# Part of one chunk of the output weights given to the first six DMA engines, with the softmax sums moved to ScalarE and four idle matmuls removed

## The chip, the cores and the metric

One Trainium2 chip, one core of it. The metric is device microseconds (us) of one execution. All numbers of runs are of executions that the record counts as fast (label2 is a single run, its state unknown); the times of one kernel are compared with runs of the kernel before made on the same chip in the same rounds. A ratio is the mean time of one kernel's fast runs over that of the other's of the same rounds, so it is not quite the ratio of the medians that are quoted beside it.

## The reference

One decode step of attention with a cached context, mixed with a gated MLP. What matters here is only the last step: the attention output `o` (32 heads of 128) times the output weights `wo`.

```python
# x: 1 x 1024;  k_cache, v_cache: 4 groups x 65536 x 128;  wo: 4096 x 1024, all bfloat16
scores = jnp.einsum('bhqd,bhkd->bhqk', q, k) * Dh ** (-0.5)
p = _softmax(scores, axis=-1)
o = jnp.einsum('bhqk,bhkd->bhqd', p, v)
a = o.transpose(0, 2, 1, 3).reshape(B, Sq, Hq * Dh) @ wo
out = g * a + (1 - g) * b          # g: a gate of x; b: the MLP branch
```

The inputs are 162 MB, each byte used once, so the kernel is a stream of loads with work hidden behind it.

## The kernel before

All loads go out from one queue (SyncE), in the order in which they are needed, into a ring of slots; a load waits until its slot has been used. The output weights come last, as four chunks of 1024 rows; the fourth is cut in three pieces so that little work is left after the last bytes.

```python
    def rows(w, i, c):          # chunk i: 128 partitions, c rows of w behind each other in each
        return w[128 * c * i:128 * c * (i + 1), :].rearrange("(p c) n -> p (c n)", c=c)
    ...
    WO_CUT = [(0, 5), (5, 7), (7, 8)]
    for i in range(3):
        load([("wo", i, 0)], rows(A_wo, i, 8), WO_AT[i])
    for c0, c1 in WO_CUT:
        load([("wo", 3, c0)], rows(A_wo, 3, 8)[:, DO * c0:DO * c1], WO_AT[3] + DO * c0)
```

The sum of the softmax of a group is a float32 product over two halves, and `spin(n)` runs n matmuls whose result nobody reads, to keep TensorE's clock up while it waits:

```python
    def out_first(g):
        def f(e):
            for h in range(2):
                ins = e.matmul(mb[:, 0:1], bm, lp[:, 2 * g + h:2 * g + h + 1], start=(h == 0), stop=(h == 1))
            return ins
    ...
    out_first(3)
    wo_rows(0)                  # chunk 0: 16 matmuls into scp
    out_rest(3)
    wo_rows(1)
    spin(4)
    spread(scp, [KSC(0)], False)   # a ScalarE copy of 1.0 us, then 16 small matmuls
    spin(3)
    wo_piece(2)                 # 64 matmuls
    spin(3)
    for c0, c1 in WO_CUT:
        wo_piece(3, c0, c1)     # 40, 16 and 8 matmuls
```

Of the kernel before, what the change touches and what calls it, by code (L numbers as in the profile page):

```python
# [8 lines left out]
ACTF = mybir.ActivationFunctionType  # L9
# [8 lines left out]
class Recorder:  # L18
# [8 lines left out]
        self.dma_count = {}  # L27
        self.ahead = 0

    def op(self, eng, fn, r=(), w=(), dma=None):  # L30
        o = Op()
        o.eng, o.fn, o.inc, o.count = eng, fn, False, 0
        o.dma = None
        deps = {}
        for k in r:
            if k in self.writer:
                deps[id(self.writer[k])] = (self.writer[k], True)
        for k in w:
            if k in self.writer:
                deps.setdefault(id(self.writer[k]), (self.writer[k], False))  # L40
            for x in self.readers.get(k, ()):
                deps.setdefault(id(x), (x, False))
        o.deps = list(deps.values())
        for k in r:
            self.readers.setdefault(k, []).append(o)
        for k in w:
            self.writer[k] = o
            self.readers[k] = []
        if dma is not None:
            self.dma_count[dma] = self.dma_count.get(dma, 0) + 16  # L50
            o.dma = (dma, self.dma_count[dma])
        o.idx = len(self.ops)
        self.ops.append(o)
        return o
# [40 lines left out]
    def emit(self, nc):  # L95
        waits = self.plan()
        sems = {e: nc.alloc_semaphore("eng_" + e) for e in self.ENGINES}
        dsem = {k: nc.alloc_semaphore("dma_%s" % k) for k in self.dma_count}
        final = {k: v for k, v in self.dma_count.items()}

        def run(eng, handle):
            for o, ws in zip(self.ops, waits):
                if o.eng != eng:
                    continue
                for d in ws:
                    if d.dma:
                        handle.wait_ge(dsem[d.dma[0]], d.dma[1])
                    else:
                        handle.wait_ge(sems[d.eng], d.count)
                last = o.fn(handle)  # L110
                if o.dma:
                    last.then_inc(dsem[o.dma[0]], 16)
                elif o.inc:
                    last.then_inc(sems[eng], 1)

        body = nc.cur_bb.bb
        gate = next(i for i, x in enumerate(body.instructions)
                    if isinstance(x, mybir.InstDrain) and x.engine == mybir.EngineType.SP)
        first = len(body.instructions)
        run("SP", nc.sync)  # L120
        nc.sync.wait_ge(dsem["out"], final["out"])
        made = list(body.instructions)
        moved = made[first:first + self.ahead]
        assert all(isinstance(x, mybir.InstDMACopy) for x in moved)
        body.instructions = made[:gate] + moved + made[gate:first] + made[first + self.ahead:]
        run("POOL", nc.gpsimd)
        run("PE", nc.tensor)
        run("ACT", nc.scalar)
        run("DVE", nc.vector)


def bass_gated_mix__gqa_block_cached__mixer_gmlp__decode_kernel(
# [19 lines left out]
    DO = A_wo.shape[1]  # L152
# [32 lines left out]

    for name, n in [
        ("RING", NSUB * SUB), ("KT", NKT * 4096), ("SC", NSC * 2048), ("PSB", 2 * 1024), ("PTSB", 2 * 1024),
        ("QPAD", 4 * QP), ("IDB", 128), ("BM", 256), ("SEL", 16 * 32),
        ("M16", 32), ("MQ", 32), ("XT", KC), ("WB", 2), ("WBB", 4), ("ONEB", 128),
        ("MAXC", 2 * total), ("LP", 2 * total), ("COLS", 2 * 64), ("DM", 64), ("ONES", 256), ("QALL", 128), ("OVZ", 32 * OC + 31), ("E4Z", 128), ("MHALF", 4),  # L190
        ("YB", FC), ("OROW", QW),
    ]:
        region(name, n)
    NA = (cur + 63) // 64 * 64
# [2 lines left out]
    def ab(name, n, o=0):  # L197
        return arena[:, OFF[name] + o:OFF[name] + o + n]

    def af(name, n, o=0):  # L200
        return arena[:, OFF[name] + 2 * o:OFF[name] + 2 * (o + n)].bitcast(F32)
# [11 lines left out]
    mhalf = af("MHALF", 2)  # L213
    yb, ovz, orow = ab("YB", FC), ab("OVZ", 32 * OC + 31), ab("OROW", QW)
    e4z = af("E4Z", 63)
    dm = af("DM", 32)
    psb, psb2 = ab("PSB", 1024), ab("PSB", 2048)
    osc, ot = ab("PSB", 512), af("PSB", 128, 256)
    col = lambda i: colt[:, i:i + 1]
# [3 lines left out]
    def gcol(g, i):  # L223
        return col(C_G4 + 12 * g + i)
# [25 lines left out]
    def mm(e, loaded, *a, **kw):  # L250

        if not loaded:
            return e.matmul(*a, **kw)  # L253
        with nc.discard():
            one = e.matmul(*a, **kw).ins  # L255
        return e.add_instruction(dataclasses.replace(one, name=nc.get_next_instruction_name(), ldweights=False))
# [7 lines left out]
    P("POOL", lambda e: e.affine_select(out=idf, in_=idf, compare_op=ALU.not_equal, fill=1.0, base=0,  # L264
                                        pattern=[[-1, 128]], channel_multiplier=1), r=["idf"], w=["idf"])
    P("POOL", lambda e: e.tensor_copy(idb, idf), r=["idf"], w=["idb"])
    P("POOL", lambda e: e.memset(qpad, 0.0), w=["qpad"])
    P("POOL", lambda e: e.memset(orow, 0.0), w=["orow"])
    P("POOL", lambda e: e.memset(ovz, 0.0), w=[("ovec", g) for g in range(G)])
    P("POOL", lambda e: e.memset(e4z, 0.0), w=["e4"])  # L270
    P("POOL", lambda e: e.memset(ones, 1.0), w=["ones"])
    P("POOL", lambda e: e.memset(oneb, 1.0), w=["oneb"])
    P("DVE", lambda e: e.memset(mb, 0.0), w=["mb"])
# [26 lines left out]
    def load(keys, src, off):  # L300

        n = len(stream)
        w = src.shape[1]
        for i, key in enumerate(keys):
            place[key] = (n, off + i * (w // len(keys)), w // len(keys))
        stream.append((keys, off, src))

    def rows(w, i, c):

        return w[128 * c * i:128 * c * (i + 1), :].rearrange("(p c) n -> p (c n)", c=c)  # L310
# [18 lines left out]
    def load_v2(n, off):  # L329
        load([("v", n), ("v", n + 1)], kv(A_v_cache, n, True), off)  # L330

    load([("wq", 0)], rows(A_wq, 0, 8), VB)
    load_k2(0, 0)
    load([("win", 0)], rows(B_w_in, 0, 8), VB)
# [13 lines left out]
    load([("v", 15)], kv(A_v_cache, 15), VB + SUB)  # L348
    WO_AT = [0, 8 * DO, 16 * DO, 24 * DO]
    WO_CUT = [(0, 5), (5, 7), (7, 8)]  # L350
    for i in range(3):
        load([("wo", i, 0)], rows(A_wo, i, 8), WO_AT[i])
    for c0, c1 in WO_CUT:
        load([("wo", 3, c0)], rows(A_wo, 3, 8)[:, DO * c0:DO * c1], WO_AT[3] + DO * c0)
# [14 lines left out]
    def issue():  # L369

        while issued[0] < len(stream):
            n = issued[0]
            keys, off, src = stream[n]
            w = src.shape[1]
            gr = grains(off, w)
            if any(k not in used for x in gr if x in owner for k in owner[x]):
                return
            for j, x in enumerate(gr):
                owner[x] = (keys[j * len(keys) // len(gr)],)
            if n == len(stream) - 1:  # L380
                store()
            P("SP", lambda e, o=OFF["RING"] + off, w=w, src=src: e.dma_start(arena[:, o:o + w], src),  # L382
              w=[("slot", x) for x in gr], dma="s%d" % gr[0])
            issued[0] += 1

    def use(key):
# [4 lines left out]
    def done(key):  # L391
        used.add(key)
        issue()
# [132 lines left out]
    def exp_pair(j):  # L526
        P("ACT", lambda e: e.activation(psb2, scs(j), ACTF.Exp, bias=gcol(j // 2, K_NB), scale=SCALE,  # L527
                                        accum_out=lp[:, j:j + 1]),
          r=[("sc", j % 2), ("nb", j // 2)], w=["psb", ("lp", j)])
# [21 lines left out]
        done(("v", n))  # L551

    def out_first(g):
        def f(e):
            for h in range(2):
                ins = e.matmul(mb[:, 0:1], bm, lp[:, 2 * g + h:2 * g + h + 1], start=(h == 0), stop=(h == 1))  # L556
            return ins
        P("PE", f, r=["bm", ("lp", 2 * g), ("lp", 2 * g + 1)], w=["mb"])

    def out_second(g):  # L560
        P("DVE", lambda e: e.reciprocal(gcol(g, K_RL), mb[:, 0:1]), w=[("rl", g), "mb"])  # L561
# [113 lines left out]
    def spin(n):  # L675
        def f(e):
            for k in range(n):
                ins = mm(e, k > 0, scp[:, 1024:1536], idb, ab("KT", 512), start=True, stop=True)
            return ins
        P("PE", f, r=["idb", ("kt", 0)], w=[KSC(1)])  # L680

    def wo_rows(i):
        sl, keys = use(("wo", i, 0))

        def f(e):
            for c in range(8):
                j = c % 4
                z = 31 + 32 * (8 * i + c)
                for s in range(2):
                    o = DO * c + 512 * s  # L690
                    ins = mm(e, s > 0, scp[32 * j:32 * j + 1, 512 * s:512 * (s + 1)], ovz[:, z:z + 1], sl[:, o:o + 512],
                             start=(i == 0 and c < 4), stop=(i == 1 and c >= 4), tile_position=(0, 32 * j),
                             skip_group_check=True)
            return ins
        P("PE", f, r=[("ovec", i)] + keys, w=[KSC(0)])
        done(("wo", i, 0))
# [24 lines left out]
    def out_rest(g):  # L721
        out_second(g)
        out_third(g)
        out_fourth(g)
# [13 lines left out]
    for i in range(6):  # L738
# [11 lines left out]
        if i % 2:  # L750
            out_rest(i // 2)
    exp_pair(7)
    for n in (12, 13, 14, 15):
        pv_piece(n)
        if n < 14:
            pt_half(n + 2)
    out_first(3)
    wo_rows(0)
    out_rest(3)
    wo_rows(1)  # L760
    spin(4)
    spread(scp, [KSC(0)], False)
    spin(3)
    wo_piece(2)
    spin(3)
    for c0, c1 in WO_CUT:
# [34 lines left out]
```

## Time and profile before

| | kernel before |
|---|---|
| median of six runs | 381.75 us (381.65 to 381.85) |
| span of the profiled execution | 380.5 us |
| share of the span: DMA data queue, PE, DVE | 98.8%, 61%, 54% |
| last bytes of data moved | 377.97 us |
| last arrival signalled | 378.39 us |

Each digit of the first line is the mean busy share of the sixteen DMA engines in a fortieth of the span, in tenths; the second line says what they moved. The queue lines give packets, megabytes and the share of sixteen engines' span. From the page of the kernel before, parts 2 and 3:

```profile
DMA  9999999999999999999999999999999999999996
GB/s 441 434 406 400 469 388 437 441 483 417 415 406 434 441 436 427 441 420 424 474 434 441 441 441 406 408 434 441 434 417 432 441 441 434 436 410 431 417 424 252
...
q1 hardware_dynamic: 4208, 162.01, 98.8%
q8 instruction: 9, 0.15, 0.2%
...
q14 instruction: 1, 0.01, 0.0%
```

The engines are busy for nine tenths or more of every slice but the last. So no wait of PE or DVE costs anything as long as it does not hold back a load, and the time is the time of the stream plus what follows its end. The nine packets of `q8` are taken to be instructions that TensorE fetches (their number fits, see below).

What follows the end is short. The end of the chain that ended last (start us, duration us, what), kernel before:

```profile
330.94 37.58 DMA arena<-in_A_wo_dram
368.53 0.04 issue
368.57 0.39 PE scp L253 x4
...
373.15 0.32 PE scp L253
373.48 0.43 PE scp L255 x2
373.91 1.90 PE fbt L705 x64
...
376.65 1.77 PE fbt L705 x56
...
378.43 0.42 PE fbt L705 x8
...
378.94 0.28 DVE arena L768
```

The last eight matmuls start 0.04 us after the last arrival. The 56 before them take 1.77 us and end 0.01 us before: PE keeps up with the data only just, at full clock. The chain also shows that PE has no break of more than 0.1 us from the arrival of chunk 1 (368.53 us) on. The granted clock stands in the sixth group of columns (PEclk) of a table of stretches, here of the kernel before:

```profile
370.00:374.00 4.00, 4.00 (x29) 1.56 (x25) 0.00 (x0) 0.70 (x1) 0.00 (x0) 0.64 0.97 404
374.00:378.00 4.00, 3.91 (x115) 3.08 (x111) 0.00 (x0) 0.00 (x0) 0.00 (x0) 1.00 0.71 284
```

From 370 to 374 us the clock is low for a part (0.64), from 374 us on full. The two spins in front of `wo_piece(2)` lie there; PE is busy for all 4.00 us.

The trace has more than the page: when each engine's share of a DMA was signalled, and start and duration of each packet.

The engines end 1.83 us apart. Eight of the nine instruction packets (16,384 bytes each) stop the data of one engine for 0.99 to 1.10 us; the ninth starts at 378.13 us, behind the last data. The data packet that follows each of the eight on its engine is slow as well, 0.47 to 0.55 us longer than others of its size, so one fetch costs its engine some 1.5 us. A single packet of 8,192 bytes at 87.69 us (the page's `q14`) takes 0.32 us, and the data packet behind it 0.66 us more than its like: together 0.98 us, as much as the arrival in between (377.52) lies behind the first. The Trainium skill says the same of their size: "Runtime: NRT & Kernel Launch", section "Instruction fetch mechanics", has instructions fetched in 16 KiB blocks of 256; this trace has nine such packets for 2285 matmul and weight-load records. The same section calls the cost of crossing a block "mostly hidden". For the stream of loads it is not: the eight late arrivals lie 1.3 to 1.8 us behind the first.

### The profile page before, as it was taken

What the parts mean: (1) busy time and instruction counts of PE and PEld (TensorE: products, weight loads), DVE (VectorE), ACT (ScalarE), POOL (GpSimd) and SP (SyncE); (2) the same over time, 40 slices, a digit from 0 to 9 for tenths busy, and PEclk for the clock granted to TensorE, in tenths of its full rate; (3) what the DMA queues carried; (4) which work ended last, traced back from release to release, by engine and by line L of the source; (5) the groups of instructions that cost most, each with busy time, mean ns of one, the idle gap of its engine ahead of it and who ended that gap; (6) DMA issues with size and microseconds to landing.
All of it is one profiled execution on the core that took longest, in us unless ns stands there. A gap on an engine that the chain in (4) does not pass through costs nothing.

```text
span 380.5 us, 2581 instructions
## 1 busy us (share of the span) xinstructions
PE 231.1 (61%) x1449; PEld 57.7 (15%) x836; DVE 204.1 (54%) x162; ACT 23.2 (6%) x24; POOL 8.4 (2%) x37
## 2 busy tenths in 40 slices
PE   0051488458548924894786128952895883738378
PEld 0010011011101200121111001220121110212015
DVE  3111596777389525955892249745875872322020
ACT  1000000010420000002100000022000000220010
POOL 5000000000000000000000000000000000000000
PEclk9998599696959985998799859995999897969789
DMA  9999999999999999999999999999999999999996
GB/s 441 434 406 400 469 388 437 441 483 417 415 406 434 441 436 427 441 420 424 474 434 441 441 441 406 408 434 441 434 417 432 441 441 434 436 410 431 417 424 252
DMA packets 4254, 162.17 MB, mean 426 GB/s; under 512 B 532, under 2 KB 532, under 8 KB 788
## 3 DMA queue, kind: packets, MB, share of 16 engines
q1 hardware_dynamic: 4208, 162.01, 98.8%
q8 instruction: 9, 0.15, 0.2%
q10 hardware_dynamic: 36, 0.00, 0.0%
q14 instruction: 1, 0.01, 0.0%
HBM read 162.01 MB, written 0.00 MB: 426 GB/s over the span
## 4 chain that ended last, share of the span: by engine, by line
DMA 57%; PE 21%; DVE 19%; ACT 1%; issue 1%; ACTq 0%; SPq 0%; DVEq 0%
DMA arena<-in_A_k_cache_dram 34%; DVE arena L495 17%; DMA arena<-in_A_wo_dram 10%; DMA arena<-in_A_v_cache_dram 8%; PE scp L253 5%; DMA arena<-in_B_b_sp_dram 5%; PE scp L255 5%; PE obt L253 4%; PE obt L255 4%; DVE arena L532 1%; PE fbt L705 1%; PE fbt L653 1%; ACT arena L527 1%; ACTq L281 0%; SPq L382 0%
## 5 line engine op out<-in xcount | busy, mean ns | idle before, releaser
L495 DVE STREAM_TRANSPOSE arena<-arena 128x2048 f32<-128x2048 f32 x64 | 142.6, 2281 | 45.4 <-DMA arena<-in_A_k_cache_dram 32.0
L253 PE MATMUL scp<-arena 128*128 128x512 bf16 (+1 forms) x275 | 110.7, 419 | 87.3 <-DVE arena L495 86.2
L255 PE MATMUL scp<-arena 128*128 128x512 bf16 (+1 forms) x279 | 110.5, 415 | 0.0
L253 PE MATMUL obt<-arena 128*64 128x512 bf16 (+2 forms) x334 | 62.3, 416 | 21.7 <-DMA arena<-in_A_v_cache_dram 20.3
L255 PE MATMUL obt<-arena 128*64 128x512 bf16 (+2 forms) x334 | 61.6, 411 | 0.0
L253 PEld LDWEIGHTS scp<-arena 128*128 128x128 bf16 (+1 forms) x275 | 27.3, 103 | 196.5 <-issue 96.9
L532 DVE STREAM_TRANSPOSE arena<-arena 128x2048 bf16<-128x2048 bf16 x7 | 16.2, 2311 | 30.1 <-PE obt L255 27.9
L253 PEld LDWEIGHTS obt<-arena 128*64 128x64 bf16 (+1 forms) x334 | 18.1, 112 | 74.3 <-issue 54.9
L527 ACT ACTIVATE arena<-arena 128x2048 bf16<-128x2048 f32 x8 | 16.0, 2002 | 218.7 <-DVE arena L524 195.8
L512 DVE TENSOR_SCALAR_CACHE_REDUCE arena<-scp 128x2048 f32<-128x2048 f32 x8 | 18.3, 2292 | 16.0 <-PE scp L255 16.0
L573 PE MATMUL mbt<-arena 128*128 128x128 bf16 x16 | 1.8, 243 | 12.6 <-DVE arena L568 12.6
L561 DVE RECIPROCAL arena<-mbt 128x1 f32<-128x1 f32 x4 | 0.6, 139 | 15.8 <-PE mbt L556 15.8
L524 DVE TENSOR_REDUCE arena<-mbt 128x1 f32<-128x32 f32 x4 | 0.8, 192 | 15.3 <-PE mbt L521 15.3
L483 POOL COPY arena<-arena 32x32 bf16<-32x32 bf16 x16 | 3.2, 203 | 235.5 <-PE scp L255 209.4
L535 DVE STREAM_TRANSPOSE arena<-arena 128x1024 bf16<-128x1024 bf16 x2 | 2.5, 1245 | 11.0 <-PE obt L255 11.0
L425 PE MATMUL scp<-arena 8*128 8x1 bf16 x8 | 0.7, 199 | 10.9 <-DVE arena L420 10.9
L430 PE MATMUL mbt<-arena 1*128 1x2 bf16 x1 | 0.2, 158 | 10.5 <-DMA arena<-in_B_b_sp_dram 10.5
L768 DVE CAST arena<-fbt 36x128 bf16<-36x128 f32 x1 | 0.3, 282 | 10.8 <-PE fbt L705 10.8
L432 DVE COPY arena<-mbt 128x2 f32<-128x2 f32 x1 | 0.2, 159 | 10.5 <-PE mbt L430 10.5
L705 PE MATMUL fbt<-arena 128*32 128x128 bf16 x128 | 4.1, 220 | 0.1
L420 DVE TENSOR_TENSOR arena<-arena 8x1024 bf16<-8x1024 bf16 x1 | 1.2, 1214 | 5.0 <-DMA arena<-in_A_x_dram 5.0
L460 DVE CAST arena<-obt 97x1024 bf16<-97x1024 f32 x1 | 1.2, 1225 | 5.0 <-PE obt L255 5.0
(91 smaller groups left out, 57.3 us busy)
## 6 DMA issues: line engine op xcount, KB each, us to landing
arena<-in_A_k_cache_dram SPq DMA_DIRECT2D x6, 4096.0 KB, 33.5
arena<-in_A_v_cache_dram SPq DMA_DIRECT2D x2, 4096.0 KB, 25.8
arena<-in_B_w_in_dram SPq DMA_DIRECT2D x1, 7168.0 KB, 29.9
arena<-in_A_wo_dram SPq DMA_DIRECT2D x3, 2048.0 KB, 33.2
arena<-in_B_w_out_dram SPq DMA_DIRECT2D x1, 3584.0 KB, 21.3
arena<-in_A_wo_dram SPq DMA_DIRECT2D x1, 1280.0 KB, 31.7
arena<-in_A_wo_dram SPq DMA_DIRECT2D x1, 512.0 KB, 32.5
arena<-in_A_wo_dram SPq DMA_DIRECT2D x1, 256.0 KB, 32.2
```

The source lines that it names most:

```text
L253: return e.matmul(*a, **kw)
L255: one = e.matmul(*a, **kw).ins
L420: P("DVE", lambda e: e.tensor_tensor(vw(xm, 0, [[128, 8], [1, 128]], 0, 8), vw(xrow, 0, [[0, 8], [1, 128]], 0, 8), vw(idb, 0, [[1, 8], [0, ...
L483: P("POOL", lambda e, pb=pb: e.tensor_copy(vw(qpad, 24 + 32 * pb, [[QP, 4], [1, 8]], 32 * pb, 32), vw(qall, 8 * g, [[32, 4], [1, 8]], 32 * ...
L495: P("DVE", lambda e: e.transpose(ktb(i).bitcast(F32), sl[:, 4096 * p:4096 * (p + 1)].bitcast(F32)), r=keys[4 * p:4 * p + 4], w=[("kt", i % ...
L512: P("DVE", lambda e: e.tensor_scalar(scs(j), scp[:, :], 0.0, None, op0=ALU.add, op1=ALU.max, accum_out=maxc[:, j:j + 1]), w=[("sc", j % 2) ...
L527: P("ACT", lambda e: e.activation(psb2, scs(j), ACTF.Exp, bias=gcol(j // 2, K_NB), scale=SCALE, accum_out=lp[:, j:j + 1]), r=[("sc", j % 2 ...
L532: P("DVE", lambda e: e.transpose(ptsb2, psb2), r=["psb"], w=[("ptsb", 0), ("ptsb", 1)])
L535: P("DVE", lambda e: e.transpose(ptsb(n), ab("PSB", 1024, 1024 * (n % 2))), r=["psb"], w=[("ptsb", n % 2)])
L573: ins = e.matmul(mb[:, 0:128], sel[:, 128 * c:128 * (c + 1)], osc[:, 128 * c:128 * (c + 1)], start=(c == 0), stop=(c == 3))
L653: ins = e.matmul(fb[32 * b:32 * (b + 1), 0:QW], e4z[0:97, 31 - j:63 - j], part[0:97, QW * s:QW * (s + 1)], start=(first and s % (NW // 2) ...
L705: ins = e.matmul(fb[32 * b:32 * (b + 1), 0:QW], ovz[:, z:z + 32], sl[:, o:o + QW], start=False, stop=(i == 3 and c == 7), tile_position=(0 ...
```

## The change

The intent is to level that spread: take work from all sixteen engines and give it to those that finish early, taken to be the first six. Half the columns (512) of one row per partition of chunk 0, 128 KB, leave the full load and come as DMAs of 24 partitions. Their source is permuted so that the outer dimension is 6. To keep TensorE's instruction stream, and with it the number of fetches, from growing by the eleven small matmuls that this needs, the two halves of each softmax sum are added on ScalarE, and four spins go. The core of the diff (cut: zero fills of the new regions merged, a counter for several DMAs on one semaphore; "..." marks other lines left out):

```diff
+    HC = 512
+    LOW = [(24 * g, 6) for g in range(5)] + [(120, 2)]
+    def load_low(key, off):
+        parts = []
+        for g, (p0, k) in enumerate(LOW):
+            src = A_wo[8 * p0:8 * (p0 + 4 * k), 0:HC].rearrange("(j i c) n -> i j c n", i=k, c=8)[:, :, 0, :]
+            o = OFF["RING"] + off + HC * g
+            parts.append((arena[0:4 * k, o:o + HC], src))
...         # the parts are put in the queue behind each other
-    for i in range(3):
+    load([("wo", 0, 0)], rows(A_wo, 0, 8)[:, HC:8 * DO], WO_AT[0] + HC)
+    load_low(("low", 0), 2 * SUB)
+    for i in range(1, 3):
         load([("wo", i, 0)], rows(A_wo, i, 8), WO_AT[i])
...
     def out_first(g):
-        def f(e):
-            for h in range(2):
-                ins = e.matmul(mb[:, 0:1], bm, lp[:, 2 * g + h:2 * g + h + 1], start=(h == 0), stop=(h == 1))
-            return ins
-        P("PE", f, r=["bm", ("lp", 2 * g), ("lp", 2 * g + 1)], w=["mb"])
+        P("ACT", lambda e: e.activation(gcol(g, K_L), lp[:, 2 * g + 1:2 * g + 2], ACTF.Identity, bias=lp[:, 2 * g:2 * g + 1]),
+          r=[("lp", 2 * g), ("lp", 2 * g + 1)], w=[("l", g)])
+        P("PE", lambda e: e.matmul(mb[:, 0:1], bm, gcol(g, K_L), start=True, stop=True), r=["bm", ("l", g)], w=["mb"])
...
+    def out_down():     # the 128 values of o for these rows, permuted as the small DMAs place their rows
+        def f(e):
+            for g in range(len(LOW)):
+                ins = e.matmul(mb[0:24, g:g + 1], perm[:, 24 * g:24 * (g + 1)], ovz[:, 31:32], start=True, stop=True)
...
+    def wo_low():
...
+            for g, (_, k) in enumerate(LOW):
+                j = g % 4
+                ins = e.matmul(scp[32 * j:32 * j + 1, 0:HC], ov0[0:4 * k, g:g + 1], sl[0:4 * k, HC * g:HC * (g + 1)], ...)
...
     out_rest(3)
+    wo_low()
     wo_rows(1)
-    spin(4)
+    spin(3)
     spread(scp, [KSC(0)], False)
-    spin(3)
     wo_piece(2)
```

## The prediction

> **What bounds the kernel.** The DMA engines. The page's slice table has DMA at 9 tenths in 39 of 40 slices, and the queue table gives the data queue 98.8% of sixteen engines' span; PE is busy 61%, DVE 54%. The chain of waits ends: last output-weight piece lands, 8 matmuls (0.42 us), a 0.28 us cast, the store. In the trace's DMA packets a 64 KB row takes 2.42 us whatever else runs: each engine moves at its own fixed rate, and the last landing is the slowest engine's.
>
> **The engines do not finish together.** The sixteen arrivals of the last piece lie at 376.56 to 376.66 us (six), 376.77, 377.52, and eight at 377.88 to 378.39. The packets show why: nine 16 KB packets of the instruction queue, about 1.0 us each; every one stops one engine's data and leaves it 1.3 to 1.8 us late. The eight before the end of data give the eight late engines; an 8 KB instruction-type packet at 87.7 us the one in between. That the early ones are engines 0 to 5 I cannot read from the trace with certainty; the diff presumes it.
>
> **What the change does.** It takes 512 columns of one row of 128 partitions (128 KB, 8 KB an engine) from the sixteen engines and gives them to the first six, as 20 to 24 rows of 1 KB each. (The Trainium skill, "DMA: Bandwidth & Descriptors", section "Why a DMA increments its semaphore by 16 and not by 1": such a DMA uses the largest k up to 16 that divides both outer dimensions, on this issue path the lowest-numbered k; 24 and 6 give 6. No run shows it yet.) From packets of 16, 10, 4 and 2 KB (615, 387, 159, 84 ns) I estimate 37 to 38 ns per KB plus 5 ns per packet: ten engines are rid of 0.30 us, six get +0.55 to +0.75 us net. The early ones have 1.6 to 1.8 us of room. The one in between, if among the six, has 0.9 us and would end about level with the shortened late ones.
>
> The rest keeps PE's instruction stream from growing: eleven small matmuls are added; four two-pass float32 matmuls go (the ScalarE sums), and four spins. By my count about zero net. This matters: the ninth instruction packet starts at 378.13 us, 0.16 us after the last data packet; some ten more PE instructions would pull it into the data. The ScalarE sums (about 0.2 us each), the permuting matmuls and the pool copies lie in idle time. The small DMAs wait for a ring slot until about 347.5 us; the queue then still holds work until 363 us: no gap.
>
> **On the critical path:** only the slowest engine's last landing, -0.25 to -0.30 us.
>
> **Predicted: 381.50 us**, 8 in 10 within 381.15 to 381.95. Faster by over 2%: 0.003; within 2%: 0.994; slower by over 2%: 0.003.
>
> **What would show it.** Arrivals of the last piece: late group about 0.3 us earlier, early group 0.55 to 0.75 us later, spread down from 1.8 us to about 1 us. Still nine instruction packets, the last after the data. No gap of the queue near 347 us. The final matmuls, cast and store as long as before.
>
> **What would make it wrong.** An instruction packet moved into the last microseconds, or onto one of the six (+0.5 us or more); the small DMAs' engines not being the early ones (+0.6 us); the granted clock, half from 369.5 to 372.9 us here, staying half through the last 128 matmuls because spins are gone (up to +1 us); 1 KB rows costing far more than estimated.

## More of the kernel before

The sixteen signals of the last weight piece, and the eight of the first output store (8 partitions; issued in front of the last piece), kernel before, us:

```
last piece  376.56 376.61 376.63 376.63 376.66 376.66 | 376.77 | 377.52 | 377.88 377.93 377.95 378.10 378.21 378.26 378.27 378.39
8-row store 376.11 376.14 376.17 376.23 376.34 | 377.09 377.52 377.84
```

## The result, and the profile after

| | before | after |
|---|---|---|
| median of six runs, us | 381.75 | 382.71 |
| lowest to highest, us | 381.65 to 381.85 | 382.00 to 384.50 |
| ratio to before | | 1.003, 95% interval 1.0008 to 1.0052 |
| span of the profiled execution, us | 380.5 | 380.9 |
| last arrival signalled, us | 378.39 | 378.77 |

Within 2%, as predicted, but slower instead of faster, and scattered. The profiled execution is one of the good ones (382.29 us). Its queue lines and the end of its chain, kernel after:

```profile
DMA  9999989999999999999999999999999999999995
...
q1 hardware_dynamic: 4368, 162.01, 98.8%
q8 instruction: 9, 0.15, 0.2%
```

```profile
355.12 21.79 DMA arena<-in_A_wo_dram
376.91 0.14 issue
377.04 1.76 PE fbt L745 x56
...
378.81 0.42 PE fbt L745 x8
...
379.32 0.28 DVE arena L809
```

The clock of the same stretches as before, kernel after; it is full from 374 us in this execution:

```profile
370.00:374.00 4.00, 3.13 (x32) 1.24 (x25) 0.00 (x0) 1.02 (x1) 0.00 (x0) 0.68 0.96 399
374.00:378.00 4.00, 3.38 (x101) 2.73 (x98) 0.00 (x0) 0.00 (x0) 0.00 (x0) 1.00 0.74 301
```

Nine instruction packets as before (matmul and weight-load records 1446 + 839, the same 2285), as many bytes of data, the same tail after the last arrival; only everything at the end is 0.38 us later. The arrivals of the last piece, kernel after, us:

```
last piece  376.04 376.10 | 376.59 377.06 377.29 377.35 377.52 377.61 377.68 377.75 377.77 377.93 378.00 378.19 | 378.37 | 378.77
```

The packets of 1 KB show whose arrivals the last two are. The six engines with small rows begin them, one after the other, at about 360.86, 360.87, 361.17, 361.30 us, and then at 362.20 and 362.57. Followed on, the last two end their data at 377.92 and 378.30, and these are the arrivals at 378.37 and 378.77. So four of the six were early and two were not. The engines without small rows did what was predicted: the last of them arrives at 378.19, 0.20 us earlier than the last of before.

### The profile page after: what moved, and what is told of

Same layout as the page of the kernel before. It is cut to its first block, busy times and chain, and to the rows that moved or that the text cites. A ratio compares the mean times of both kernels' runs of the same rounds, so it can differ in the third digit from the quotient of the medians.

```text
span 380.9 us, 2590 instructions
## 1 busy us (share of the span) xinstructions
PE 234.7 (62%) x1446; PEld 57.6 (15%) x839; DVE 204.6 (54%) x163; ACT 24.1 (6%) x28; POOL 8.9 (2%) x36
## 4 chain that ended last, share of the span: by engine, by line
DMA 53%; PE 23%; DVE 19%; SPq 1%; ACT 1%; issue 1%; ACTq 0%; DVEq 0%
DMA arena<-in_A_k_cache_dram 33%; DVE arena L514 16%; DMA arena<-in_A_v_cache_dram 9%; PE scp L254 7%; PE scp L256 6%; DMA arena<-in_A_wo_dram 6%; DMA arena<-in_B_b_sp_dram 5%; PE obt L254 4%; PE obt L256 4%; DVE arena L551 2%; SPq L401 1%; PE fbt L745 1%; ACT arena L546 1%; ACTq L284 0%; PE fbt L670 0%
## 5 line engine op out<-in xcount | busy, mean ns | idle before, releaser
L254 PE MATMUL scp<-arena 128*128 128x512 bf16 (+1 forms) x272 | 112.2, 432 | 86.9 <-DVE arena L514 85.4
L256 PE MATMUL scp<-arena 128*128 128x512 bf16 (+1 forms) x275 | 112.9, 432 | 0.5 <-issue 0.5
L254 PE MATMUL obt<-arena 128*64 128x512 bf16 (+2 forms) x334 | 63.0, 420 | 16.8 <-DMA arena<-in_A_v_cache_dram 16.8
L256 PE MATMUL obt<-arena 128*64 128x512 bf16 (+2 forms) x334 | 62.3, 415 | 0.0
L745 PEld LDWEIGHTS fbt<-arena 128*32 128x32 bf16 x128 | 3.6, 97 | 2.2 <-issue 1.2
```

What stands on the lines that cost most here:

```text
L254: return e.matmul(*a, **kw)
L256: one = e.matmul(*a, **kw).ins
L745: ins = e.matmul(fb[32 * b:32 * (b + 1), 0:QW], ovz[:, z:z + 32], sl[:, o:o + QW], start=False, stop=(i == 3 and c == 7), tile_position=(0 ...
```

## The experiments

Two theories. E (engines): the premise is wrong, some of engines 0 to 5 are late ones, and the small rows make these later still. C (clock): without the spins, TensorE's half-granted clock reaches into the last 128 matmuls in some executions. Rivals: a cost of the ScalarE sums, or of the small matmuls. Thirteen runs were made, all correct (again and label2 repeat a kernel).

| run | what differs | median (range), us | before, same rounds |
|---|---|---|---|
| again | the changed kernel | 382.38 (382.27 to 383.32) | 381.84 (381.58 to 382.01) |
| wide | its 512 columns over all sixteen engines | 381.97 (381.95 to 382.79) | the same |
| spins | changed, spins back | 382.28 (382.12 to 382.38) | the same |
| sums | before, ScalarE sums alone | 381.82 (381.75 to 381.93) | the same |
| label | before, with marks of 4 bytes | 381.75 (381.68 to 381.88) | 381.79 (381.70 to 381.94) |
| wspin | wide, spins back | 381.89 (381.81 to 382.05) | the same |
| nosums | changed, without the sums | 382.67 (382.35 to 383.10) | the same |
| half | 256 columns on six engines, spins back | 382.03 (381.92 to 382.34) | 381.83 (381.61 to 381.96) |
| two | 256 columns, engines 0 and 1, one DMA | 382.08 (381.84 to 382.18) | the same |
| four | 256 columns, engines 0 to 3, one DMA | 382.14 (381.92 to 385.16) | the same |
| label2 | label once more | 381.72 (one run) | the same |
| three | 384 columns, engines 0 to 2, spins back | 381.68 (381.59 to 381.81) | 381.83 (381.65 to 382.14) |
| nospin | before, the change's spins alone | 381.74 (381.70 to 382.71) | the same |

**again.** No edit.

> The changed kernel once more, for its spread and a second trace. Theory E (engines): the 1 KB rows go to engines 0 to 5, two of which are already late in the first trace (an instruction packet before the rows, an 8 KB packet at 85.5 us), so the last landing is again an engine of the six, ending about 0.4 us later than the last landing of before or more; time 382.0 to 384.5 us, spread over 1 us, against 0.2 us for before. Theory C (clock): the spread comes from the half-granted clock in the last 128 matmuls, so slow executions show a lower mean clock than fast ones of the same kernel. Under E the mean clock says nothing about the time.

Three executions at 382.27 to 382.38, two at 383.3. The mean clocks listed are 0.839 for both of the slow ones, but also for two of the good ones, so that mark of theory C fails: a mean over the span does not tell. The place of the clock does. The profiled execution is a slow one (383.32); its stretches, then its timeline (start, duration, engine, line, operation, shapes, and in brackets the idle time before):

```profile
370.00:374.00 4.00, 1.84 (x22) 0.90 (x17) 0.00 (x0) 1.02 (x1) 0.00 (x0) 1.00 0.98 411
374.00:378.00 4.00, 3.62 (x66) 2.98 (x65) 0.00 (x0) 0.00 (x0) 0.00 (x0) 0.57 0.74 300
```

```profile
374.04 3.14 PE L745 MATMUL fbt<-arena 128*32 128x128 bf16 x64 [1.66 <-DMA arena<-in_A_wo_dram]
377.11 0.10 PEld L254 LDWEIGHTS scp<-arena 128*128 128x128 bf16 x1 [0.20 <-issue]
377.51 0.84 PE L256 MATMUL scp<-arena 128*128 128x512 bf16 x2 [0.33 <-issue]
...
378.29 1.96 PE L745 MATMUL fbt<-arena 128*32 128x128 bf16 x64
380.36 0.28 DVE L809 CAST arena<-fbt 36x128 bf16<-36x128 f32 x1 [11.54 <-PE fbt L745]
```

PE was busy for 1.84 of the 4 us before 374 us, where before was busy throughout (in part because at half clock the same matmuls take longer), and then had 0.57 of its clock where before had 1.00. The 64 matmuls of chunk 2 take 3.14 us; in the kernel before the same 64 take 1.96:

```profile
373.84 1.96 PE L705 MATMUL fbt<-arena 128*32 128x128 bf16 x64
```

Chunk 3's matmuls therefore start at 378.29 instead of on arrival, and end behind the last arrival (378.96 us) instead of with it. The last eight matmuls start 0.90 us behind that arrival, not 0.04. That is the second level, some 1.0 us above the first: 383.3 against 382.3. The Trainium skill, "TensorE: Matmul & The Clock Gate", section "Part 1: The HAM clock gate", says that the clock follows a free-running window of 3413 ns; the clock events of this trace lie that way, half from 374.59 to 378.00 us, and in the kernel before from 369.46 to 372.87, both 3.41 us. Where the half window falls differs between executions: in the kernel after it lay at 369.17 to 372.58 us, in front of the last 128 matmuls. An idle PE alone does not bring it: in the traces of wide and nosums PE was as idle from 370 to 374 us (1.85 and 2.16 us busy) and the clock stayed full. If windows of 3.41 us run on from the last clock event before this stretch (364.35 us here, 364.85 and 364.83 in those two), the idle one began at 371.18 us here and 0.5 us later in those two, so that theirs took in more of chunk 2's matmuls; this fits the phase as the cause and does not prove it. In the kernel before none of 44 timed executions lies more than 0.5 us over the lowest of its rounds.

**wide.** The same columns as one DMA of 128 partitions; five of the six small matmuls get zero weights, so their count stays.

```diff
-            parts.append((arena[0:4 * k, o:o + HC], src))          # six small DMAs
+        parts = [(arena[:, o:o + HC], rows(A_wo, 0, 8)[:, 0:HC]),
+                 (arena[0:6, o + HC:o + HC + 2], A_wo[0:6, 0:2]), (arena[0:1, ...], A_wo[0:1, 0:2])]   # marks
```

> The 512 columns loaded as one DMA of 128 partitions over all sixteen engines (8 KB each) at the place of the six small ones, with two DMAs of a few bytes that mark engines 0 to 5 and engine 0 in the trace; matmul count, spins and ScalarE sums as in the changed kernel. Theory E: time of before, 381.65 to 381.95 us, and a spread of 0.3 us or less. Theory C or a cost of the ScalarE sums: as slow and as scattered as the changed kernel, 382.0 to 384.5 us.

Four of five at 381.95 to 382.00, one at 382.79. The small matmuls are all still there, so they are not the loss. The loss of the good executions is nearly gone and the outlier has stayed: two causes, not one. About 0.1 us over before is left; an extra row packet for each partition and the marks may be a part of it; this was not looked into.

**spins.**

```diff
-    spin(3)
+    spin(4)
     spread(scp, [KSC(0)], False)
+    spin(3)
```

> The changed kernel with the four spins back (4 and 3 instead of 3 and 0). Theory C: time of before or better, 381.4 to 381.9 us. Theory E: still 382.0 us or more, median within 0.5 us of the changed kernel; five more PE instructions may bring the ninth instruction packet 0.1 us nearer to the data and make it worse still.

All five within 0.26 us, no second level, and all slower than the slowest run of before, by 0.44 us in the mean (the interval of the ratio, 0.9999 to 1.0024, just takes in 1). In its trace the last arrival is at 378.77, as in the kernel after. So with the spins the outliers are gone and the loss is not; five executions alone would not prove it, the count under nospin adds to it: theory C accounts for the scatter, theory E is left for the 0.44.

**sums.** The kernel before with the changed `out_first` alone.

> The kernel before with the ScalarE sums alone (four float32 matmuls fewer, eight or more PE instructions fewer). All theories of mine: within 0.15 us of before, 381.6 to 381.9 us, same spread. If the sums carry a cost of their own (rival S): 382.0 us or more.

Equal to before. The sums cost nothing.

**label.** The kernel before, and behind chunk 0 seven DMAs on 1 to 7 partitions, two elements each:

```diff
+            stream.append(((("probe", 0),), 2 * SUB, GRAN,
+                           [(arena[0:k, o + 16 * k:o + 16 * k + 2], A_wo[0:k, 0:2]) for k in range(1, 8)]))
```

> The kernel before, with seven DMAs of 4 bytes a partition on 1 to 7 partitions behind the first output-weight chunk: engine 0 gets seven of them, engine 1 six, engine 6 one, so the trace tells the engines apart. Theory E: two of engines 0 to 5, and not all six early, reach their marks over 0.9 us after the first; engines with marks 6 and 5 (0 and 1) early, since the rows of 24 packets were early in three traces of the changed kernel. Time of before within 0.15 us. If all of 0 to 5 are early here, theory E falls.

The trace shows a row of 4-byte packets behind each engine's last chunk-0 packet, 15, 13, 11, 9, 7, 5 and 3 long (a semaphore packet, and two for each mark). So a DMA on k partitions uses k engines, and each set holds the smaller ones. That these are the lowest-numbered is what the Trainium skill says ("DMA: Bandwidth & Descriptors", section "Why a DMA increments its semaphore by 16 and not by 1"); the trace has no engine numbers, and those used here are counted by the marks. The times of the first packet of each, us, in this run and in label2:

```
engine      0       1       2       3       4       5       6
label    361.13  361.27  361.29  362.49  361.29  362.80  362.73
label2   361.29  361.30  361.42  362.46  361.59  362.76  362.90
```

This is the premise of the change, measured, and it does not hold: of engines 0 to 5, four are early, engine 3 is 1.2 to 1.4 us and engine 5 1.5 to 1.7 us behind engine 0. The small rows go to both.

**wspin.** wide, with the spins of the run spins.

> The wide load and the four spins back: what is left of the change is the permuting and ScalarE work and six small matmuls. Theory E for the 0.45 us and theory C for the outliers: 381.6 to 381.95 us in all five executions, none above 382.3. If an outlier near 382.8 or 383.3 appears again, the spins are not what it hangs on.

No outlier in five. Between wide and wspin there is the same step as between again and spins.

**nosums.** The changed kernel with the old `out_first`.

> The changed kernel without the ScalarE sums, so 8 PE instructions more. My account in the prediction: the ninth instruction packet starts some 0.1 to 0.2 us earlier and falls into the data of the last engines; if it hits one of those still at work, the time rises by up to 1 us over the changed kernel. If it hits an engine that is done: no change, 382.2 to 382.4 us, with the same outliers near 383.3.

As slow and scattered as the changed kernel. The eighth packet came 3.3 us earlier than in the changed kernel (367.31 against 370.58), the ninth not at all earlier (378.42 against 378.32), because PE waited for later data; it stopped no engine that was still at work. The last arrival of its trace is at 379.12, 1.04 us behind the next: the engine with the last small rows began them at 362.90 us, 2.0 us after the first, and no instruction packet came behind that. Why it was later still than in the kernel after is open. My account of what the sums are for is not confirmed by this run; it is not refuted either.

**half.** `HC = 256`, spins back (and the other 256 columns of that row computed last in `wo_rows(0)`).

> 256 instead of 512 columns over engines 0 to 5, with the four spins back. From the label run engine 5 is among the latest (1.68 us behind the first) and takes 20 rows. Theory E, worked out from the packets (1 KB rows every 42 ns, so 512 B rows some 24 ns): every engine is rid of 0.15 us, engine 5 gains 0.33 us net, the last landing moves by about +0.15 us or so against before, +0.2 us less than in the changed kernel with spins: 381.9 to 382.1 us. If the loss does not shrink with the dose (382.25 us or more), it is not the rows on engine 5.

The median is 0.20 us over before, against 0.44 for the full dose, and the last arrival of its trace is at 378.51, 0.12 later than before. Half the dose, half the loss, within the noise. (The clock in this execution's records is at most 0.85; the last matmuls still started 0.05 us after the last arrival.)

**two and four.** One DMA in place of the small ones; with an outer dimension of 2 or 4 only so many engines carry it. It writes all 128 partitions.

```diff
+        src = A_wo[0:1024, 0:HC].rearrange("(j i c) n -> i j c n", i=LK, c=8)[:, :, 0, :]     # LK = 2 or 4
+        parts = [(arena[:, OFF["RING"] + off:OFF["RING"] + off + HC], src)]
```

> 256 columns as ONE DMA of 128 partitions whose source has an outer dimension of 2, so that only engines 0 and 1 carry it (64 rows of 512 B each, about +1.4 us net; both are 1.6 to 1.8 us early by the label run); spins back. If what limits an engine is the engine: the last landing 0.15 us earlier than before, 381.6 to 381.7 us. If it is the side it writes to (engines 0 and 1 now write partitions that other engines also write), the gain vanishes or turns: 381.8 us or more.

> The same 256 columns as one DMA with an outer dimension of 4: engines 0 to 3 carry 32 rows of 512 B each (about +0.6 us net). Engine 3, late by 0.9 to 1.1 us from the 8 KB packet, still has 0.7 us of room. Expected as for two: 381.6 to 381.7 us if the engine limits, 381.8 us or more if the side written to.

Neither gains. In the trace of two, packets of 16 KB that start from 361 to 363 us take 692 ns in the mean over all engines (614 in the kernel before, the same window); the longest of the run takes 828. In half, with rows of the same 512 bytes but each engine writing its own partitions, the mean is 629 ns. So most of the rise goes with writing partitions that other engines write too. The Trainium skill ("DMA: Bandwidth & Descriptors", "Where 436 GB/s comes from") calls the sixteen ports of the on-chip memory (SBUF) the bottleneck; this run fits that and does not show a port. For the changed kernel it means that writing partitions 0 to 23 was a right choice: each of engines 0 to 5 writes there only what it also writes in a full load (section "The descriptor swizzle"). One execution of four took 385.16 us, with a mean clock of 0.708 and a granted clock of at most 0.75 in its records; the profiled execution of half, at most 0.85, is the only other traced one that never had the full clock. The loads were slow in it too, long before the small rows: many 64 KB packets from 143 to 157 us took 0.1 to 1.0 us longer than the usual 2.42. It is left unexplained.

**label2.** label again, another execution and another chip.

> The marked kernel again in another execution. If the instruction packets take the same engines each time: engines 0, 1, 2, 4 early, 3 late by 0.9 to 1.4 us, 5 and 6 by 1.4 to 1.7 us, as before. If the engines change with the execution, other marks are late.

The same engines are late. In all traces of kernels with six small DMAs that I followed (after, again, spins, nosums) four engines begin their small rows early, one about 1.0 to 1.4 us and one 1.7 to 2.0 us after the first. The assignment did not change between executions here.

**three.** Small rows only for engines 0, 1 and 2, and only into partitions they write in full loads (0 to 11 and 32 to 43): ten DMAs of 12 partitions and one of 8, 384 columns, spins back.

```diff
-    HC = 512
+    HC = 384
-    LOW = [(24 * g, 6) for g in range(5)] + [(120, 2)]
+    LOW = [(24 * g, 3) for g in range(5)] + [(120, 2)]
+            for h in range(2 if k == 3 else 1):
+                r = p0 + 12 * h
+                parts.append((arena[32 * h:32 * h + 4 * k, o:o + HC], src))      # src from row r
```

> 384 columns over engines 0, 1 and 2 alone, in eleven DMAs of 12 (or 8) partitions, each engine writing only partitions that it also writes in the full loads; spins back. Theory E with the side-written limit: sixteen engines are rid of 0.22 us, engines 0 to 2 gain about 1.3 us net and stay in front of the last, so the last landing is 0.2 us earlier than before and the time 381.5 to 381.65 us. If it is 381.8 us or more, early engines have no usable room and the idea is dead; a longer queue of small issues before the second chunk could also eat it (then a gap in the data near 362 us).

The end of the chain, kernel three:

```profile
376.37 1.81 PE fbt L751 x56
...
378.20 0.42 PE fbt L751 x8
...
378.72 0.28 DVE arena L816
```

The last arrival is at 378.16, 0.23 us earlier than before, and the last eight matmuls and the cast follow, each 0.22 to 0.23 us earlier than in the lines of before. No gap in the data. The times are 381.68 against 381.83 in the median, the ratio 0.9996 with an interval of 0.9984 to 1.0009: the trace shows an earlier end, the times agree with it and by themselves do not prove a gain. Nor is one trace proof: the last arrival of nospin, with no small DMA, lies 0.27 us later than that of before. But 378.16 is the earliest of all fifteen traces; in the others without rows for chosen engines it lies at 378.31 to 378.66. And eleven small DMAs, more than the change had, cost nothing measurable once they were on early engines: it is not the number of them that hurt.

**nospin.** The kernel before with `spin(3)` and none instead of `spin(4)` and `spin(3)`.

> The kernel before with the change's spins (3 and none) and nothing else. Theory C: most executions at 381.6 to 381.9 us, but one or two of five higher by 0.7 to 1.1 us, with the half clock between about 373 and 378 us in the trace if the profiled one is such. If all five stay under 382.0 us, the outliers need more than the missing spins (or are rarer than I think).

Four between 381.70 and 382.07, one at 382.71. The outlier appears without any small DMA. (Its profiled execution is the one of 382.07, with a full clock at the end and one engine 0.37 us behind the next; the outlier itself has no trace.) Over all runs, kernels without the four spins (after, again, wide, nosums, nospin) have executions 0.7 us or more over their own lowest in 8 of 25; those of the changed kernels with them (spins, wspin, half, two, three, four) in 1 of 31, the 385.16 us of four; the kernel before in none of 44. Only one of the eight, in again, has a trace that shows the half clock.

## Why the prediction was wrong

- **What bounds the kernel: right.** The slowest engine's last arrival sets the time: the last eight matmuls start 0.04 or 0.05 us after it in thirteen of the fifteen traces, all but again (0.90) and the slow one of four (0.36). The arrivals of label, half and three differ by -0.02, +0.12 and -0.23 us from before, their median times by -0.04, +0.20 and -0.15. That PE is on the path too, from chunk 1 on, was not said; it changed nothing here, as all arrivals of the slow engine moved together (chunk 1 by +0.38 us as well).
- **That late engines are relieved of about 0.30 us: right in kind, a little large.** The last engine without small rows is 0.20 us earlier.
- **"The early ones have 1.6 to 1.8 us of room": this step failed.** The sentence was true of the early engines, and the sum then took the six engines of the small DMAs to be these. Engine 5 had an estimated 0.2 to 0.4 us of room instead (1.47 and 1.67 us behind engine 0 in the marked runs, out of a spread of 1.83 us), and was loaded with about 0.58 us net: twenty rows of 1 KB take 0.88 us in the trace (362.57 to 363.45), less the estimated 0.30. So it had to end 0.2 to 0.4 us later than the last of before. The term "-0.25 to -0.30 us" on the critical path measured +0.38 us. Engine 3, the one in between, behaved about as I said it might: it ended 0.18 us behind the shortened late ones.
- **It could have been read before.** The output store has eight rows, one for each of engines 0 to 7, and its arrivals in the trace of before are five early and three late. With three late ones among eight, at least one of any six of them is late. I named the wrong set of engines as a risk ("+0.6 us") and still gave it no weight in the range.
- **The spins: the second failed term.** I wrote that the half clock might stay through the last matmuls, up to +1 us, as a thing that could go wrong. It is about +1.0 us in the traced execution of again, a second of its five has the same time, and the three slow runs of six lift the median to 382.71, between the two levels. One run of 384.5 us has no trace and stays open.
- **The instruction stream: right.** The records of PE are 2285 in both, nine packets in both. That this needed the ScalarE sums was not shown (nosums).
- **The cost of the small rows and the queue without a gap: right.** The rows follow each other every 42 ns; 42 to 43 were estimated.

## What to carry to other kernels

When a stream of loads bounds a kernel, look at the spread of one DMA's sixteen arrivals: the last one counts, and instruction fetches alone set engines 1.3 to 1.8 us apart here. Before work is given to the engines thought early, mark them: a few DMAs of 4 bytes on 1, 2, 3 ... partitions cost nothing measurable and name each engine in the trace. Matmuls that do nothing may be what keeps the clock up; take them out only with several executions timed, since the harm comes in a part of them.

## What the Trainium skill lacked or had wrong

- "Runtime: NRT & Kernel Launch", "Instruction fetch mechanics": the cost of crossing a 16 KiB block is called mostly hidden, and what it costs the DMA engine that carries the block is not mentioned. In this kernel, bound by loads, a packet of 16,384 bytes stops one engine's data for 0.99 to 1.10 us, the data packet behind it takes 0.47 to 0.55 us longer than its like, and the engine ends 1.3 to 1.8 us behind.
- No page says which of the sixteen engines the fetches fall on. In the marked runs engines 0, 1, 2 and 4 were early and 3, 5 and 6 late by 1.2 to 1.7 us, the same in two executions on two chips; engine 3, by its smaller lag, probably after the one packet of 8,192 bytes at 85 to 88 us (0.98 us in the kernel before).
- "DMA: Bandwidth & Descriptors", "The descriptor swizzle" and "Where 436 GB/s comes from": they do not say what follows when an engine writes another's partitions. In run two, 16 KB packets took 692 ns in the mean of the window, against 614 in the kernel before and 629 in half, where no engine did that.
- "TensorE: Matmul & The Clock Gate" puts the cost of the ramp under 1% of a typical span. The share holds here (1.0 of 382 us), but the page gives no case of one kernel whose executions differ at their end by whether a half-clock window falls into the last matmuls: 8 of 25 executions without the four idle matmuls are 0.7 us or more over the lowest of their kernel, 1 of 31 of changed kernels with them (one traced case shows the window).
